# One core, threshold attention and a GELU MLP: eight sums moved forward, one transpose for two heads, and three small moves

## The chip, the cores and the metric

The kernel runs on one core of a Trainium2 chip. A core has a matrix engine (TensorE, PE in the profile; its weight loads are PEld and overlap the matmuls), VectorE (DVE), ScalarE (ACT), GpSimd (POOL), SyncE (SP, which here only issues transfers), and 16 DMA engines that move data between DRAM and the on-chip memories SBUF and PSUM (TensorE writes only to PSUM). Each engine works through its own queue in order, and semaphores hold an instruction back until what it needs is there. The metric is device time in microseconds, as a median of several executions.

## The reference

Inputs are q, k, v of 8 batches x 8 heads x 576 rows x 64, a scalar tau, and two weight matrices.

```python
scores = scale * np.matmul(q, k.transpose(0, 1, 3, 2))        # scale = 1/8
thresh = np.max(scores, axis=-1, keepdims=True) - tau
scores = np.where(scores >= thresh, scores, -1000000000.0)
attn = np.exp(scores - np.max(scores, axis=-1, keepdims=True))
attn = attn / (np.sum(attn, axis=-1, keepdims=True) + 1e-09)
attn_out = np.matmul(attn, v)
x = attn_out.transpose(0, 2, 1, 3).reshape(4608, 512)         # tokens x (head, channel)
h = x @ w_in                                                  # w_in 512 x 2048
g = 0.5 * h * (1.0 + erf(h / sqrt(2)))
out = g @ w_out                                               # w_out 2048 x 512
```

The two weight matrices arrive as 8-byte floats, and the kernel itself brings them to 4 bytes. All matmuls are in 4-byte floats.

## The kernel before, in words

**Slots.** The attention is cut into 32 pairs of heads (four pairs are a batch), and each pair into five chunks of 128 query rows (the fifth has the last 64 rows of both heads). A (pair, chunk) is a slot; there are 160, numbered n. The first 20 slots are the "early" ones: pairs 0 to 3 with chunks 0 and 1 first (n below 8), then chunks 2 to 4 of the same pairs. After them each pair runs through its five chunks. The engines' queues are written out by hand in this order; no scheduler reorders them.

What a slot does: TensorE makes the scores (L355); VectorE takes each row's maximum (L367, reading PSUM); GpSimd forms the threshold (L368); ScalarE the exponential (L370); VectorE compares, multiplies and sums (L386). An early slot then forms reciprocals of the row sums (L389 on GpSimd, L397 on VectorE), puts them on diagonals (L400, ScalarE), and TensorE turns the probabilities by multiplying with these diagonals (L301, one slot later). A later slot turns them on VectorE, in 32 x 32 blocks, with one instruction for each head (L433), into the tiles pd[0] and pd[1], and SyncE's transfers regroup these blocks (L444 for the tail, L448). Divisors are turned by VectorE, sent to DRAM and fetched back, spread over the partitions ("turned", "inv", L408 to L421). TensorE multiplies the turned probabilities with v (L460), one pair later, and VectorE divides while it takes the result out of PSUM (L478).

**The weights' conversion.** There are 32 pieces of 128 x 512. A piece is fetched by GpSimd's queue in two transfers (raw, L154, and the same shifted by three bytes, L156). VectorE takes out the exponent (expo, L176), ScalarE makes a power of two from it (L177), and VectorE does three more steps (mant L183, power L185, and L187, which writes w_in or w_out and behind which the next piece's load is issued). The steps are a generator; VectorE works at one piece's expo ahead of the piece before it. At the end of each slot it goes on until a budget in ns is used up: 3000 in each of the first 8 slots, 3650 up to slot 18, and all that is left in slot 19. Two pieces are loaded before the first slot, two more behind the first chunk of pairs 0 and 1. Odd pieces are fetched into free room of pd[0] and pd[1], even ones into tiles of the pool xg.

**The MLP.** Tokens go in 18 blocks of 256. The first ten are done plainly: h in PSUM (L520), GELU (L500, before which ScalarE loads the GELU table; L507 is a small Exp that brings the Exp table back), the second product (L532), a copy (L535) and a store (L537). Their matmuls fill the slots' gaps on TensorE, by a running goal of blocks done.

**The last eight blocks** are done behind the last slot as four duos, two blocks each, by Strassen's scheme in Winograd's form: 7 products of half-size blocks (L641) instead of 8, with sums and differences of quarters formed by VectorE. The weights' sums come in two parts. `weights_in` (L592 to L594) makes twelve sums out of w_in when the last slot is done, into tiles that are free by then. `strassen`, called when the last pair's products with v and all plain blocks are in the queues, begins with four differences that overwrite quarters of w_in (L612), and then with the four sums of the first duo's tokens (`x_sums`, L653 to L656). Those overwrite the quarter b12 of the second block, and write three new tiles (x_ext). Then, for each of eight chunks of the hidden dimension, TensorE makes the products of the w_in side and VectorE and ScalarE take them out. w_out's quarter sums (L661 to L664) are made inside the first duo. The second products follow, and their results are stored 128 rows x 512 columns at a time (L744, L749) by SyncE. Results are put together in lo (tiles of tag o_sb, n1's rows) and hi (o_ext, n2's rows); each holds two column halves, finished at different times.

**The front.** The program's last part begins with the transfers of pairs 0 and 1: `load_early` puts q's on SyncE's queue and k's, for these two pairs, on ScalarE's, which then turns to L278 and L280, where it copies the turned q and k out of PSUM. The first Exp table is loaded by ScalarE in front of L278.

Of the kernel before, what the change touches and what calls it, by code (L numbers as in the profile page):

```python
# [18 lines left out]
def kernel(  # L19
# [69 lines left out]

    ident = const.tile([P, P], FP32, name="ident")  # L90
# [5 lines left out]
    pd = [const.tile([P, 4 * KR, P], FP32, name=f"pd{e}") for e in range(2)]  # L96
# [326 lines left out]
    def turn_p(p, i):  # L423

        s = st[p]
        w = s.pop(("p", i))
        n = 1 if i == NC else 2  # L430
        for e in reversed(range(n)):
            to = pd_tail[p % 2] if i == NC else pd[e][:, :, i * Q:(i + 1) * Q]
            nc.vector.transpose(to[:, 0:NB, :], w[:, e * S:(e + 1) * S].rearrange("p (b i) -> p b i", i=Q))  # L433
# [58 lines left out]
    warm = const.tile([P, 2], FP32, name="warm")  # L492
    nc.vector.memset(warm, 0.0)

# [15 lines left out]
    def block_steps(n):  # L510

        g = {}
        for j in range(N_DF):
# [11 lines left out]
        for m in range(TOK // P):  # L525
            for j in range(N_DF):
                yield NS_OUT, len(pieces) - N_DF + j + 1
                if j not in g:
                    gelus(0)
                if j == 0:  # L530
                    o = ps.tile([P, 512], FP32, tag="mm", name="o_ps")
                nc.tensor.matmul(o[:, 0:d_model], lhsT=g[j][:, m * P:(m + 1) * P], rhs=w_out_sb[j],  # L532
                                 start=(j == 0), stop=(j == N_DF - 1))
# [5 lines left out]
    mlp = {"n": 0, "steps": None, "next": None, "debt": 0.0}  # L539
# [41 lines left out]
    def weights_in():  # L581
# [3 lines left out]
        rest = [units(v_sb[i % 4])[0] for i in range(NP - 4, NP - 1)]  # L585
# [9 lines left out]
        return (s1, s2, s4), room + rest  # L595
# [11 lines left out]
    def strassen(ext, room):  # L607
        s1, s2, s4 = ext
        for h in range(HF // U):
            for c in range(NK):  # L610
                a = w_in_sb[c][:, HF + h * U:HF + (h + 1) * U]
                vec.tensor_tensor(a, w_in_sb[c][:, h * U:(h + 1) * U], a, op=ALU.subtract)  # L612
        room = room + units(v_sb[(NP - 1) % 4]) + [u for t in pd_tail for u in units(t)]
        room += [x for _ in range(2) for x in unit(xg, "x", 2)]
        x_ext = [room.pop().rearrange("p (c t) -> p c t", c=NK) for _ in range(3)]
# [33 lines left out]
        def x_sums(n1, n2):  # L649
            t1, t2, t4 = x_ext  # L650
            a, b = x_blk[n1], x_blk[n2]
            b11, b21, b12, b22 = a[:, 0:NK, :], a[:, NK:2 * NK, :], b[:, 0:NK, :], b[:, NK:2 * NK, :]
            vec.tensor_tensor(t1, b12, b11, op=ALU.subtract)  # L653
            vec.tensor_tensor(t2, b22, t1, op=ALU.subtract)
            vec.tensor_tensor(b12, b22, b12, op=ALU.subtract)  # L655
            vec.tensor_tensor(t4, b21, t2, op=ALU.subtract)  # L656

# [7 lines left out]

        def finish_chunk(j, x, p3):
# [6 lines left out]
        x_sums(*DUOS[0])  # L673
        for sb, (n1, n2) in enumerate(DUOS):
# [45 lines left out]
            for m in ms:  # L720
# [3 lines left out]
                vec.tensor_tensor(lo[m][:, 0:HD], lo[m][:, 0:HD], vs[m], op=ALU.add)  # L724
            for n in DUOS[sb + 1] if sb + 1 < len(DUOS) else ():
                if n in away:
                    bring(n)
            if sb + 1 < len(DUOS):
                x_sums(*DUOS[sb + 1])
# [7 lines left out]
            for m in ms:  # L737
                product(ys[m], rows(g22, m, wt4))
                vec.tensor_tensor(hi[m][:, 0:HD], hi[m][:, 0:HD], ys[m], op=ALU.add)
            for m in ms:  # L740
                product(xs[m], rows(gs1, m, wt1))
                vec.tensor_tensor(hi[m][:, HD:2 * HD], hi[m][:, HD:2 * HD], xs[m], op=ALU.add)
                row = n2 * TOK + m * P
                nc.sync.dma_start(out[row:row + P, :], hi[m])  # L744
            for m in ms:
                product(xs[m], rows(g12, m, w_out_part(1, 1)))
                nc.scalar.copy(lo[m][:, HD:2 * HD], xs[m])
                row = n1 * TOK + m * P
                nc.sync.dma_start(out[row:row + P, :], lo[m])  # L749

    load_early(0)
    load_early(1)
# [32 lines left out]
    for n in range(len(slots) + WEIGH + 1):  # L785
# [60 lines left out]
        convert(3000 if n < 2 * HP else 3650 if n < BATCH - 1 else 1e9)  # L846
# [54 lines left out]
```

## Time and profile before

| | |
|---|---|
| median of 7 executions | 1430.25 us (1425.93 to 1433.08) |
| the profiled execution | 1426.63 us, of which 1424.5 is its span |
| mean granted clock of TensorE in it | 0.993 |
| TensorE busy | 1379.0 us, 97% of the span |
| VectorE busy | 899.3 us, 63% |
| ScalarE busy | 639.8 us, 45% |
| GpSimd busy | 387.1 us, 27% |
| chain that ended last | TensorE 84%, VectorE 7%, ScalarE 5%, DMA 2% |
| VectorE's transposes, L433 | 224 of 128 x 576, mean 756 ns, 160.7 us |
| VectorE's maxima, L367 | 288, mean 748 ns |
| ScalarE's table loads | 1283 ns each |

How to read it: times are of one execution, in microseconds from the start of the span unless marked ns. In a row, `out<-in` are the program's tile names, then come partitions x elements and the type; `x2` counts merged instructions of one form, which may overlap in time. A bracket such as `[3.24 <-DVE x L655]` is the time that the engine stood idle in front of the row, and what ended it. "Waits" are idle times summed by what ended them. The slices are fortieths of the span, 35.6 us each, and their digits are tenths. A share is a mean over stages with different limits, so what an edit is worth has to be read at its own place.

### The profile page before, as it was taken

Reading aid. Unit: us, or ns where it says so; the run is one execution under the profiler, and the core shown is the slowest. Engines: PE = TensorE matmul, PEld = TensorE weight load, DVE = VectorE, ACT = ScalarE, POOL = GpSimd, SP = SyncE. Lnnn points to the kernel's source line nnn. Section 1 sums busy time; section 2 is a strip of 40 time slices with the busy share of each in tenths; the row PEclk is TensorE's granted clock in tenths of the full one; section 3 lists DMA queues with packets and bytes.
Section 4 is the critical chain, followed back from the end, with each engine's and each line's share of the span. In section 5 each row is a group of like instructions: output and inputs, shape, how many; then the busy total and the mean of one; then the engine's idle time right before and its main releaser. Section 6 shows DMA issues by size and latency. Waiting matters only on the chain.

```text
span 1424.5 us, 19776 instructions
## 1 busy us (share of the span) xinstructions
PE 1379.0 (97%) x6544; PEld 956.9 (67%) x6544; DVE 899.3 (63%) x1908; ACT 639.8 (45%) x1039; POOL 387.1 (27%) x810
## 2 busy tenths in 40 slices
PE   5898899999999999999999999999999999999999
PEld 4676557466475564655746657466488888888887
DVE  5987687777767777777777777777664142241330
ACT  5768535446255373562735627457141141230320
POOL 4443244343334434334334344330000000000000
PEclk8999999999999999999999999999999999999999
DMA  9978267776667776677767777765500100100000
GB/s 267 294 264 241 55 142 150 154 144 126 136 142 143 155 139 140 141 142 162 155 136 144 161 157 149 142 134 101 107 0 1 45 1 0 60 1 8 23 1 30
DMA packets 449492, 167.06 MB, mean 117 GB/s; under 512 B 413040, under 2 KB 432048, under 8 KB 449392
## 3 DMA queue, kind: packets, MB, share of 16 engines
q1 hardware_dynamic: 423184, 108.65, 39.0%
q0 software_dynamic: 23808, 56.57, 13.2%
q8 instruction: 53, 0.87, 0.3%
q10 hardware_dynamic: 2400, 0.59, 0.2%
q14 instruction: 47, 0.39, 0.1%
HBM read 71.68 MB, written 11.47 MB: 58 GB/s over the span
## 4 chain that ended last, share of the span: by engine, by line
PE 84%; DVE 7%; ACT 5%; DMA 2%; issue 1%; SPq 0%; POOL 0%; DVEq 0%; ACTq 0%; POOLq 0%
PE bank L641 27%; PE hT L520 18%; PE o_ps L532 18%; PE sc L355 12%; PE xT L460 9%; DVE p L386 2%; ACT p L370 2%; DVE nmx L367 1%; DVE power L185 1%; ACT L500 1%; DVE w_in L187 1%; ACT diag L400 1%; DVE expo L176 1%; DVE mant L183 0%; PE tr L301 0%
## 5 line engine op out<-in xcount | busy, mean ns | idle before, releaser
L370 ACT ACTIVATE p<-sc,nmx 128x576 f32<-128x576 f32 x288 | 202.3, 738 | 384.2 <-DVE nmx L367 384.1
L367 DVE TENSOR_REDUCE nmx<-sc 128x1 f32<-128x576 f32 x288 | 204.8, 748 | 146.6 <-PE sc L355 146.6
L520 PE MATMUL hT<-x,w_in 128*128 128x256 f32 x1280 | 296.2, 384 | 0.0
L532 PE MATMUL o_ps<-w_out,g 128*128 128x512 f32 x640 | 294.2, 602 | 0.0
L520 PEld LDWEIGHTS hT<-x,w_in 128*128 128x128 f32 x1280 | 238.4, 190 | 56.9 <-issue 25.2
L386 DVE SCALAR_TENSOR_TENSOR p<-sc,thr,p 128x576 f32<-128x576 f32 x288 | 225.2, 815 | 65.4 <-ACT p L370 64.3
L368 POOL TENSOR_SCALAR thr<-nmx,tau_eff 128x1 f32<-128x1 f32 x288 | 84.1, 292 | 545.2 <-DVE nmx L367 542.6
L532 PEld LDWEIGHTS o_ps<-w_out,g 128*128 128x128 f32 x640 | 116.6, 190 | 140.3 <-issue 138.6
L355 PE MATMUL sc<-kT,qT 64*128 64x288 f32 x960 | 164.9, 432 | 2.6 <-DVE p L386 2.3
L460 PE MATMUL xT<-pT,v 128*64 128x288 f32 (+2 forms) x1280 | 164.0, 409 | 3.2 <-ACT g L500 3.2
L433 DVE STREAM_TRANSPOSE pd<-p 128x576 f32<-128x576 f32 x224 | 160.7, 756 | 3.0
L355 PEld LDWEIGHTS sc<-kT,qT 64*128 64x128 f32 x960 | 93.1, 187 | 84.3 <-issue 71.8
L460 PEld LDWEIGHTS xT<-pT,v 128*64 128x64 f32 x1280 | 89.9, 137 | 73.2 <-issue 13.1
L232 POOL DMA_DIRECT2D v<-in_v_dram x208 | 110.5, 534 | 10.5 <-issue 9.5
L641 PE MATMUL bank<-x,w_in 128*128 128x256 f32 x384 | 94.5, 382 | 3.2 <-DVE x L655 3.2
L500 ACT ACT_TABLE_LOAD x71 | 91.1, 1283 | 1.2
L507 ACT ACT_TABLE_LOAD x71 | 91.1, 1283 | 1.2
L641 PE MATMUL bank<-unit 128*128 128x256 f32 x352 | 88.4, 381 | 0.0
L641 PEld LDWEIGHTS bank<-x,w_in 128*128 128x128 f32 x384 | 73.4, 191 | 14.0 <-issue 4.1
L223 POOL DMA_DIRECT2D q<-in_q_dram x104 | 70.6, 684 | 15.7 <-issue 14.8
L641 PEld LDWEIGHTS bank<-unit 128*128 128x128 f32 x352 | 67.4, 192 | 9.4
L641 PE MATMUL bank<-w_out,unit 128*128 128x256 f32 x320 | 72.3, 379 | 0.0
(143 smaller groups left out, 1316.9 us busy)
## 6 DMA issues: line engine op xcount, KB each, us to landing
pT<-pd SPq DMA_DIRECT2D x448, 160.0 KB, 3.9
pT<-pd_tail SPq DMA_DIRECT2D x112, 80.0 KB, 2.8
q<-in_q_dram POOLq DMA_DIRECT2D x104, 72.0 KB, 4.0
k<-in_k_dram POOLq DMA_DIRECT2D x104, 72.0 KB, 2.6
out_dram<-o_sb SPq DMA_DIRECT2D x28, 256.0 KB, 3.9
inv<-turned SPq DMA_DIRECT2D x56, 128.0 KB, 4.1
v<-in_v_dram POOLq DMA_DIRECT2D x156, 40.0 KB, 3.1
raw<-in_moe_w_in_dram POOLq DMA_DIRECT2D x8, 512.0 KB, 6.4
```

Of the source, the lines that this page charges most:

```text
L232: eng.dma_start(t[r:P:4, e, 0:n, :], rows[:, r * KR:r * KR + n, :])
L355: nc.tensor.matmul(sc[e][:, h, 0:HALF], lhsT=lhsT, rhs=s["kT"][rows, at:at + HALF], start=True, stop=True)
L367: nc.vector.tensor_reduce(nmx[:, e:e + 1], sc, axis=AXIS.XY, op=ALU.max, negate=True)
L370: nc.scalar.activation(w[:, e * S:(e + 1) * S].rearrange("p (h s) -> p h s", h=2), sc, AF.Exp, bias=nmx[:, e:e + 1], scale=1.0)
L386: nc.vector.scalar_tensor_tensor(row, sc[e][:, :, 0:HALF], thr[:, e:e + 1], row, op0=ALU.is_ge, op1=ALU.mult, accum_out=den[e])
L433: nc.vector.transpose(to[:, 0:NB, :], w[:, e * S:(e + 1) * S].rearrange("p (b i) -> p b i", i=Q))
L460: nc.tensor.matmul(xT[f, 0:hi - lo], lhsT=s["v"][:, e, c, :], rhs=pT[:, c, lo:hi], start=(c == 0), stop=(c == KR - 1))
L500: nc.scalar.activation(t, hT, AF.Gelu)
L507: nc.scalar.activation(warm[:, 1:2], warm[:, 0:1], AF.Exp)
L520: nc.tensor.matmul(hT[:, j % 2, :], lhsT=w_in_sb[c][:, j * P:(j + 1) * P], rhs=x_blk[n][:, c, :], start=(c == 0), stop=(c == N_DM - 1))
L532: nc.tensor.matmul(o[:, 0:d_model], lhsT=g[j][:, m * P:(m + 1) * P], rhs=w_out_sb[j], start=(j == 0), stop=(j == N_DF - 1))
L641: nc.tensor.matmul(to, lhsT=l, rhs=r, start=start and k == 0, stop=k == len(pairs) - 1, skip_group_check=not start)
```

## The change

Five edits:

1. `pd[0]` and `pd[1]` become two views of one tile, `turned_p`, and `turn_p` turns both heads by one VectorE instruction over 128 x 1152 instead of two over 128 x 576 (the fifth chunk, with one, stays).
2. The four differences that overwrite quarters of w_in and the first duo's four token sums move from the beginning of `strassen` into `weights_in`, directly behind its twelve sums. The tiles x_ext are taken from v's tiles of three of the last four pairs instead of from the end of the list of free room. An assertion says that the last plain block is by then in its second product, so that nothing still reads w_in. `x_sums` becomes a function of its own.
3. A small Exp, with which its table is loaded, is put on ScalarE's queue between the transfers of pair 0 and those of pair 1; the tile that it uses is set to zero at the very beginning.
4. The conversion's budget is 0 in slot 0 and 3400 in slots 1 to 7 (before: 3000 in slots 0 to 7).
5. In `strassen` each result is stored in two halves of 256 columns, each as soon as it is complete, instead of one row block of 512 columns.

```diff
+    warm = const.tile([P, 2], FP32, name="warm")
+    nc.vector.memset(warm, 0.0)
...
-    pd = [const.tile([P, 4 * KR, P], FP32, name=f"pd{e}") for e in range(2)]
+    turned_p = const.tile([P, 2, 4 * KR, P], FP32, name="turned_p")
+    pd = [turned_p[:, e, :, :] for e in range(2)]
...
-        n = 1 if i == NC else 2
-        for e in reversed(range(n)):
-            to = pd_tail[p % 2] if i == NC else pd[e][:, :, i * Q:(i + 1) * Q]
-            nc.vector.transpose(to[:, 0:NB, :], w[:, e * S:(e + 1) * S].rearrange("p (b i) -> p b i", i=Q))
+        if i == NC:
+            nc.vector.transpose(pd_tail[p % 2][:, 0:NB, :], w[:, 0:S].rearrange("p (b i) -> p b i", i=Q))
+            return
+        nc.vector.transpose(
+            turned_p[:, :, 0:NB, i * Q:(i + 1) * Q], w.rearrange("p (e b i) -> p e b i", e=2, i=Q))
...
     def weights_in():
...
-        rest = [units(v_sb[i % 4])[0] for i in range(NP - 4, NP - 1)]
+        x_ext = [units(v_sb[i % 4])[0].rearrange("p (c t) -> p c t", c=NK) for i in range(NP - 4, NP - 1)]
...
-        return (s1, s2, s4), room + rest
...
-    def strassen(ext, room):
-        s1, s2, s4 = ext
+        assert mlp["n"] == PLAIN and mlp["layer"] == 2
         for h in range(HF // U):
             for c in range(NK):
                 a = w_in_sb[c][:, HF + h * U:HF + (h + 1) * U]
                 vec.tensor_tensor(a, w_in_sb[c][:, h * U:(h + 1) * U], a, op=ALU.subtract)
+        x_sums(x_ext, *DUOS[0])
+        return (s1, s2, s4), x_ext, room
...
+    def strassen(ext, x_ext, room):
+        s1, s2, s4 = ext
...
-        x_ext = [room.pop().rearrange("p (c t) -> p c t", c=NK) for _ in range(3)]
...
+        def store(n, m, t, at):
+            row = n * TOK + m * P
+            nc.sync.dma_start(out[row:row + P, at:at + HD], t[:, at:at + HD])
...
-        x_sums(*DUOS[0])
...
                 vec.tensor_tensor(lo[m][:, 0:HD], lo[m][:, 0:HD], vs[m], op=ALU.add)
+                store(n1, m, lo[m], 0)
...
                 vec.tensor_tensor(hi[m][:, 0:HD], hi[m][:, 0:HD], ys[m], op=ALU.add)
+                store(n2, m, hi[m], 0)
...
                 vec.tensor_tensor(hi[m][:, HD:2 * HD], hi[m][:, HD:2 * HD], xs[m], op=ALU.add)
-                row = n2 * TOK + m * P
-                nc.sync.dma_start(out[row:row + P, :], hi[m])
+                store(n2, m, hi[m], HD)
...
                 nc.scalar.copy(lo[m][:, HD:2 * HD], xs[m])
-                row = n1 * TOK + m * P
-                nc.sync.dma_start(out[row:row + P, :], lo[m])
+                store(n1, m, lo[m], HD)
 
     load_early(0)
+    nc.scalar.activation(warm[:, 1:2], warm[:, 0:1], AF.Exp)
     load_early(1)
...
-        convert(3000 if n < 2 * HP else 3650 if n < BATCH - 1 else 1e9)
+        convert(0 if n == 0 else 3400 if n < 2 * HP else 3650 if n < BATCH - 1 else 1e9)
```

## The prediction

> **What bounds the kernel now.** I read the page's forty slices first, then the waits of TensorE, then the order of time around the two places where TensorE stands. All durations are of the profiled execution, 1426.63 us with a span of 1424.5; it lies 3.6 us under the median of the seven runs (1430.25). The sum is made on 1426.63 and the 3.6 is added back at the end. A change of less than 0.2%, 2.9 us, is about what a measurement of this kernel cannot tell from none.
>
> The slices of the page, tenths of busy time and of the granted clock:
>
> ```profile
> PE   5898899999999999999999999999999999999999
> DVE  5987687777767777777777777777664142241330
> PEclk8999999999999999999999999999999999999999
> ```
>
> TensorE is full from slice 6 on; VectorE is at 9 only in the first slices. The table of 25 us windows says the same: VectorE 23.36 us of 25 in 50 to 75 us, some 19 from 200 to 1000. So what saves VectorE time after 200 us saves nothing, unless TensorE is seen waiting. The waits of TensorE from 200 us to the end:
>
> ```profile
> PE bank L641 <- DVE x L655: 3.2, 1, 3.2
> PE xT L460 <- ACT g L500: 3.2, 2, 1.6
> PE bank L641 <- DVE pd L697: 2.1, 4, 0.5
> PE sc L355 <- DVE p L386: 1.4, 6, 0.2
> ```
>
> Of 9.9 us, only the first line is touched by the change.
>
> **The quarter sums.** The timeline where the last pair ends:
>
> ```profile
> 1019.19 0.69 DVE L594 TENSOR_TENSOR unit<-w_in,unit 128x512 f32<-128x512 f32 x1
> ...
> 1024.82 0.95 DVE L478 TENSOR_TENSOR x<-xT,inv 128x64 f32<-128x64 f32 x4 [4.93 <-DMA inv<-turned]
> ...
> 1025.68 2.48 DVE L612 TENSOR_TENSOR w_in<-w_in 128x512 f32<-128x512 f32 x4
> ...
> 1029.42 0.69 DVE L655 TENSOR_TENSOR x<-x 128x512 f32<-128x512 f32 x1
> ...
> 1030.25 2.04 PE L641 MATMUL bank<-x,w_in 128*128 128x256 f32 x4 [3.24 <-DVE x L655]
> ...
> 1032.09 1.71 PE L641 MATMUL bank<-unit 128*128 128x256 f32 x4
> ...
> 1034.50 1.03 PE L641 MATMUL bank<-x,w_in 128*128 128x256 f32 x4
> ```
>
> VectorE ends the weight sums at 1019.9, stands 4.93 us for the divisors' transfer, divides, and only then makes the four differences of w_in (L612, 2.48 us) and the four token sums (L653 to L656, from 1028.09 to 1030.7, 2.6 us). TensorE's second product waits for L655. The change puts these eight operations behind L594: 1019.9 + 2.5 + 2.6 = 1025.0. The one TensorE needs is over at 1024.3, and TensorE asks for it at 1026.9, so 2.6 us are to spare. They lie in the 4.93 us that VectorE stood still; the four divisions behind them start at 1025.0 instead of 1024.8, and the PSUM banks that they free are asked for again only in the second chunk, after 1031. TensorE loses no 3.24 us. It also loses no slow stretch: after the gap four matmuls took 2.04, then 1.71 us, against 1.03 later. By starts, 1030.25 to 1033.64 holds eight matmuls, 3.39 us, where eight of the steady rate take 1.72 (0.86 from start to start of four): 1.67 more. Term: 3.2 + 1.7 = **-4.9 us**, between -3.2 (the slow stretch comes anyway) and -5.2. What is late next is the steady loop, in which each of the rows above is under 0.5 us.
>
> The Trainium skill, "TensorE: Matmul & The Clock Gate", section "What's actually happening", gives half clock after at least one idle window of about 3.4 us. The gap here is 3.24 us and the rows behind it run at half rate; read strictly the rule would leave the clock alone and the whole sum would be 1.7 us smaller. The row decides.
>
> **No conversion in slot 0.** The timeline of the front:
>
> ```profile
> 16.94 0.69 DVE L185 SCALAR_TENSOR_TENSOR power<-raw,power 128x512 uint32<-128x512 uint32 x1 [1.48 <-ACT power L177]
> ...
> 20.17 0.43 DVE L176 TENSOR_SCALAR expo<-raw 128x512 uint32<-128x512 uint32 x1 [1.81 <-DMA raw<-in_moe_w_in_dram]
> ...
> 20.93 1.40 DVE L367 TENSOR_REDUCE nmx<-sc 128x1 f32<-128x576 f32 x2
> ...
> 25.14 0.61 POOL L154 DMA_DIRECT2D raw<-in_moe_w_in_dram  x1
> ...
> 30.81 0.44 DVE L176 TENSOR_SCALAR expo<-raw 128x512 uint32<-128x512 uint32 x1
> ```
>
> VectorE waits 1.48 and 1.81 us inside slot 0's conversions, and slot 1's scores, ready at about 15.9 (L355, 14.89 + 1.31), are first read at 20.93. Without the conversions L367 of slot 1 starts at 15.9, five us earlier. Slot 1's softmax takes 20.93 to 24.38, 3.45 us: 19.35. Then the 3400 of slot 1 are eight steps: expo, expo, mant, power, w_in, expo, mant, power. Starts lie 0.34, 0.34, 0.34, 0.61, 0.69, 0.34, 0.34, 0.61 apart, 3.6 us, and some 0.3 of waiting for ScalarE: slot 2's L367 at 23.3, against 27.71. That is 4.4 us early, but five steps (w_in, expo, mant, power, w_in: 2.7 us) are still owed that were done before: 1.7 ahead.
>
> Now the loads. Piece 4 was issued inside slot 1 (25.14, landed 4.6 us later, a number of the DMA view for that issue) and used at 30.81, unwaited. In the changed program three loads stand together behind slot 2's L389 on GpSimd, piece 4 first, and VectorE wants piece 4 at the end of the same slot. Slot 2's softmax ends at 23.3 + 3.1 = 26.4 (27.71 to 30.81 before), L389 takes 0.6, issue at 27.1, landing at 31.7. VectorE arrives after w_in, expo, mant, power, w_in at 29.1 and stands **2.6 us**; queued behind it are slot 2's reciprocal and slot 3's maximum, and ScalarE's diagonal and TensorE's transposes wait for these. Slot 3's L367 starts at 32.3 against 33.60: 1.3 early, with expo, mant, power and w_in (2.0 us) owed. These are paid in slots 3 to 7, where VectorE has no room (23.36 of 25 us). Term: **+0.7 us**. Bounds: without the stand, -1.9; with the slowest landing of such a load in the front (8.9 us, issue at 46.22), +5.0. I take 4.6 because the loads with 7 to 9 us stood in line behind another piece, which piece 4 would not.
>
> **Table at the front.** One load and its small Exp move ahead of pair 1's three k loads on ScalarE's queue.
>
> ```profile
> 6.21 1.28 ACT L278 ACT_TABLE_LOAD   x1 [6.21 <-DMA k<-in_k_dram]
> ...
> 7.51 0.69 ACT L278 ACTIVATE qT<-tr,q_scale 128x512 f32<-128x512 f32 x1
> 8.28 0.58 ACT L280 COPY kT<-tr 128x512 f32<-128x512 f32 x1
> ```
>
> L278 may start at 7.39 instead of 7.51, but L280 waits for TensorE's transposes until 8.26 either way: 0. Pair 1's k goes out 1.5 us later (4.0 instead of 2.5); its last part, behind q's loads as before, lands near 14.5, when the scores' banks come free (14.45). 0, between -0.1 and +1.
>
> **One transpose for two.** 112 pairs of 1.44 us (mean 756 ns, overlapping) become 112 of 1.2 to 1.5; a 512-wide one takes 678 ns, so the price goes with the elements. On VectorE after 160 us this is covered by TensorE. SyncE's first regroup load of a group now waits for both halves, 0.7 us. In a steady pair sixteen loads run without a gap (207.9 to 224.2), the last tail load is out at 227.4, landed at about 230, and TensorE's second half of L460 starts at 234.7: covered by over 4 us. Only in the last pair (sixteen from 997.6 to 1013.6, tail out at 1017.9, second half at about 1019.9) nothing is to spare: +0.3, between 0 and +0.7.
>
> **Stores by halves.** Sixteen more issues on an idle SyncE. Only the last counts: 128 KB instead of 256 KB.
>
> ```profile
> out_dram<-o_sb SPq DMA_DIRECT2D x2, 256.0 KB, 2.0
> turned<-turned SPq DMA_DIRECT2D x28, 16.0 KB, 2.0
> ```
>
> By these rows size does not matter and the gain is 0; the bytes of the last store fill two slices of 0.525 us in the DMA view, so half of at most 1.05 is the other end. I take -0.3. "DMA: Bandwidth & Descriptors" of the skill ("Measured") asks for batches of 1 MiB and more, which speaks against halves; the sum is the same by it, since no other store is on the path.
>
> **Sum:** -4.9 + 0.7 + 0 + 0.3 - 0.3 = -4.2: 1422.4 on the profiled execution, 1426.0 in the median's frame.
>
> **The rivals.** *A, the front pays too.* Piece 4 lands before VectorE asks for it, because the piece ahead left the queue free. For it: 1.48 + 1.81 us of idle time are really gone. Against: 27.1 + 4.6 is after 29.1. Then -1.9 instead of +0.7: 1423.4. *B, the front is starved.* The DMA engines are at 1.04 and 0.94 of their time from 25 to 75 us, and loads that start later land later (7.1 and 8.9 us are in the rows). Then +3 to +5 instead of +0.7, and 1428.3 to 1430.3: no change to tell. *C, slower: the wide transpose.* If one pattern over both heads costs more per element, VectorE, which has 6 of 25 us free, some 1.5 us a slot, fills up. It decides from 1.44 + 1.5 = 2.9 us; at 3.2 each of 112 slots adds 0.3 and TensorE waits in L355: +34 - 4, about 1460. For it: no row shows this shape; against: the rate of the rows goes with the elements. *D, the sums do not help,* because the compiler's waits hold L655 back to the divisions: 1426.0 + 4.9 = 1430.9; against: nothing they read is written by the divisions.
>
> **How the numbers follow.** My case 0.46, A 0.18, B 0.22, C 0.08, D 0.06. The likeliest case alone reaches from 1424 to 1428. The range 1421.0 to 1431.0 takes in A less 2.4 us of scatter, and B and D whole; C and the tails, some 0.15, are left out. Faster by over 0.2% (under 1427.4): 0.85 of mine (0.39), A, a little of B (0.03): 0.60. Within: the rest of mine (0.07), most of B (0.14), D (0.06): 0.27. Slower (over 1433.1): C, and 0.05 of B, should several loads land late: 0.13.
>
> **What would show it.** Right: no wait for the token sums at the first block products and no matmuls at half rate there (PE at 1.03 us per four at once); slot 1's maximum at about 16 us; a wait of 2 to 3 us for raw at about 29 to 32; slot 3's maximum at 32 to 33. Wrong: slot 8's maximum (65.42 before) more than 2 us away from that; a transpose row over 1.6 us; TensorE waiting between 200 and 1000 us for anything longer than before.

## The result and the profile after

The changed kernel takes 1435.2 us (median of 16 executions, 1432.67 to 1442.02) where the kernel before takes 1429.46 (40 executions): a ratio of 1.0046, 95% interval [1.0037, 1.0055], which is 6.6 us slower (the two medians lie 5.7 us apart). The prediction was 1426.0, at least 1421 and at most 1431: faster than before.

The profiled execution took 1433.68 us, its span 1431.9. It lies 1.5 us under its kernel's median, the profile of before (1426.63) 2.8 us under 1429.46, so what is read between the two profiles is 1.3 us larger than between the medians. The slices of the page after, for the three engines' rows that the prediction showed:

```profile
PE   6898899999999999999999999999999999999999
DVE  4887777777777777777777767777754132241330
PEclk9899999999999999999999999999999999999999
```

Nothing is seen at this grain but a VectorE that is less full at the front. The waits of TensorE from 200 us to the end say more:

```profile
PE sc L358 <- DVE p L389: 4.6, 8, 1.8
PE xT L464 <- ACT g L501: 3.2, 2, 1.6
PE bank L655 <- DVE turned_p L705: 2.1, 4, 0.5
PE xT L464 <- DMA pT<-pd_tail: 0.9, 1, 0.9
PE xT L464 <- issue: 0.6, 1, 0.6
```

The wait for the token sums (3.2 us) is gone, as forecast. New are 3.2 us more of waiting for scores' banks, and 1.5 us for the last pair's tail. Where the time went is best read from when each slot's first maximum starts (L367 before, L370 after), after less before:

| slot (pair, chunk) | us |
|---|---|
| 1 (0, 1) | -2.2 |
| 3 (1, 1) | +2.2 |
| 8 (0, 2) | +6.6 |
| 107 (21, 2) | +6.4 |
| 110 (22, 0) | +8.1 |
| 125 (25, 0) | +8.4 |
| 130 (26, 0) | +11.0 |
| 159, the last | +10.7 |
| end of the span | +7.4 |

So the end gained 3.3 us, and 10.7 were lost before it: 6.6 in the first eight slots, and the rest, in two jumps, in pairs 21 and 25. Of the 6.6 a part is scatter: three kernels below with the front of the kernel before untouched (sums_only, turn_only, halves_only) start slot 8 at 66.9 to 67.3 us, where the profile of before has 65.42.

The timeline of the front, after:

```profile
16.26 0.36 PE L286 MATMUL tr<-ident,k 64*128 64x64 f32 x1 [1.41 <-DMA k<-in_k_dram]
...
18.69 1.42 DVE L370 TENSOR_REDUCE nmx<-sc 128x1 f32<-128x576 f32 x2 [3.80 <-PE sc L358]
...
25.86 1.40 DVE L370 TENSOR_REDUCE nmx<-sc 128x1 f32<-128x576 f32 x2
...
35.38 0.43 DVE L179 TENSOR_SCALAR expo<-raw 128x512 uint32<-128x512 uint32 x1 [3.72 <-DMA raw<-in_moe_w_in_dram]
...
35.80 1.40 DVE L370 TENSOR_REDUCE nmx<-sc 128x1 f32<-128x576 f32 x2
```

TensorE's queue waits for pair 1's k before it comes to slot 1's scores; VectorE, with no conversions to do, stands 3.80 us. It stands again, 3.72 us, for the piece whose load was forecast to be late.

The jump in pair 21, on SyncE and VectorE, before and then after:

```profile
685.11 0.59 SPq L413 DMA_DIRECT2D turned<-turned  x1
687.05 0.60 SPq L419 DMA_DIRECT2D inv<-turned  x1
...
693.27 0.52 DVE L478 TENSOR_TENSOR x<-xT,inv 128x192 f32<-128x192 f32 x2 [0.87 <-DMA inv<-turned]
```

```profile
693.30 0.58 SPq L416 DMA_DIRECT2D turned<-turned  x1
697.35 0.59 SPq L422 DMA_DIRECT2D inv<-turned  x1
...
703.62 0.52 DVE L482 TENSOR_TENSOR x<-xT,inv 128x192 f32<-128x192 f32 x2 [4.78 <-DMA inv<-turned]
...
707.51 1.42 DVE L370 TENSOR_REDUCE nmx<-sc 128x1 f32<-128x576 f32 x2
```

Taken from the pair's slot, the store of pair 20's divisors is issued 1.8 us later than before (693.30 less 685.11 and less the 6.4 of the front), their fetch 3.9 us later. VectorE's division waits 4.78 us, and behind it on its queue stand the transpose and the next slot's maximum, for which TensorE waits. The table of 200 to 1000 us (busy us of the engines, then granted clock, the 16 DMA engines' busy share, GB/s) has the same bytes moved in both, but not in the same time; before and then after:

```profile
200.00:1000.00 800.00, 795.38 (x3713) 487.77 (x3712) 604.19 (x1240) 407.31 (x540) 308.31 (x637) 1.00 0.71 143
```

```profile
200.00:1000.00 800.00, 792.09 (x3674) 485.18 (x3673) 594.06 (x1128) 403.85 (x538) 308.50 (x637) 1.00 0.77 144
```

The share went from 0.71 to 0.77: the transfers themselves became slower. No step of the prediction has a place for that.

### The profile page after: what moved, and what is told of

It is laid out like the page before. It is cut to its first block, busy times and chain, and to the rows that moved or that the text cites. A ratio compares the mean times of both kernels' runs of the same rounds, so it can differ in the third digit from the quotient of the medians.

```text
span 1431.9 us, 19665 instructions
## 1 busy us (share of the span) xinstructions
PE 1384.7 (97%) x6544; PEld 959.3 (67%) x6544; DVE 892.2 (62%) x1796; ACT 639.9 (45%) x1040; POOL 386.8 (27%) x810
## 4 chain that ended last, share of the span: by engine, by line
PE 83%; DVE 7%; ACT 5%; DMA 3%; issue 1%; SPq 1%; POOL 0%; DVEq 0%; ACTq 0%; POOLq 0%
PE bank L655 27%; PE hT L522 17%; PE o_ps L535 17%; PE sc L358 12%; PE xT L464 9%; ACT p L373 2%; DVE p L389 2%; PE tr L304 1%; DVE nmx L370 1%; DVE power L188 1%; ACT L501 1%; DMA k<-in_k_dram 1%; DVE w_in L190 1%; ACT diag L403 1%; DMA turned<-turned 1%
## 5 line engine op out<-in xcount | busy, mean ns | idle before, releaser
L370 DVE TENSOR_REDUCE nmx<-sc 128x1 f32<-128x576 f32 x288 | 204.8, 748 | 136.8 <-PE sc L358 136.6
L436 DVE STREAM_TRANSPOSE turned_p<-p 128x1152 f32<-128x1152 f32 x112 | 154.1, 1376 | 3.2 <-DVE x L482 0.2
L235 POOL DMA_DIRECT2D v<-in_v_dram x208 | 110.6, 534 | 10.7 <-issue 10.0
L655 PE MATMUL bank<-x,w_in 128*128 128x256 f32 x384 | 93.3, 379 | 0.0
L655 PE MATMUL bank<-w_out,unit 128*128 128x256 f32 x416 | 92.4, 379 | 0.0
L655 PEld LDWEIGHTS bank<-w_out,unit 128*128 128x128 f32 x416 | 79.0, 190 | 10.7
L655 PEld LDWEIGHTS bank<-x,w_in 128*128 128x128 f32 x384 | 73.0, 190 | 10.3 <-issue 0.5
L304 PE MATMUL tr<-diag,p 128*128 128x128 f32 (+1 forms) x360 | 50.5, 306 | 22.9 <-ACT diag L403 13.9
```

The lines of the kernel that those rows point to most:

```text
L235: eng.dma_start(t[r:P:4, e, 0:n, :], rows[:, r * KR:r * KR + n, :])
L370: nc.vector.tensor_reduce(nmx[:, e:e + 1], sc, axis=AXIS.XY, op=ALU.max, negate=True)
L436: nc.vector.transpose(turned_p[:, :, 0:NB, i * Q:(i + 1) * Q], w.rearrange("p (e b i) -> p e b i", e=2, i=Q))
L655: nc.tensor.matmul(to, lhsT=l, rhs=r, start=start and k == 0, stop=k == len(pairs) - 1, skip_group_check=not start)
```

## The experiments

All ratios are to the kernel before, timed in the same session, with 95% intervals; differences in us are worked out from the ratio. "Share" is the busy share of the 16 DMA engines from 200 to 1000 us.

### Each part alone

**sums_only**: the eight sums moved, nothing else.

```diff
-        return (s1, s2, s4), room + rest
+        for h in range(HF // U):
+            ...  (the four differences of w_in, from strassen)
+        x_sums(x_ext, *DUOS[0])
+        return (s1, s2, s4), x_ext, room
```

> The kernel before, with the four differences and the first duo's token sums moved behind the twelve weight sums, and nothing else. Theory (the parts' effects are separate, and the changed kernel's loss lies elsewhere): no wait for the token sums in front of the first block products and no matmuls at half rate there, -4 to -5 us, ratio 0.9965 to 0.9972; the distance from the last pair's first maximum to the end of the span shrinks by as much. Rival (the eight sums crowd out something of the last pair, whose tail is seen 1.5 us later in the changed kernel): -3.4 us or less, and TensorE waits for the regrouped tail there, as in the changed kernel (0.9 us for pd_tail).

0.9972 [0.9959, 0.9985], -4.0 us. The wait for L655 is gone, the first eight products run at full rate (1.89 us for eight), and from the last slot's maximum to the end of the span there are 411.6 us instead of 416.6: -5.0. The rival's crowding is not there: the last 40 products with v run in one row.

**slot0_only**: no conversion in slot 0.

```diff
-        convert(3000 if n < 2 * HP else 3650 if n < BATCH - 1 else 1e9)
+        convert(0 if n == 0 else 3400 if n < 2 * HP else 3650 if n < BATCH - 1 else 1e9)
```

> The kernel before, with no conversion in slot 0 and 3400 in slots 1 to 7. Theory (two causes in the front: the fifth piece's load is issued too late, and the table's place makes pair 1's k late): the k part is missing here, so slot 1's maximum starts at 16 to 17 us and not at 18.7; VectorE still stands 3 to 4 us for the fifth piece in slot 2; slot 8's maximum 3.5 to 4.5 us later than before, the time +3.5 to +4.5 us, ratio 1.0025 to 1.0031. Rival (all of the front's loss is the missing conversion, the table costs nothing): slot 8 6 us later, ratio 1.004 or more.

1.0031 [1.0016, 1.0046], +4.4 us. Slot 1's maximum starts at 16.23, slot 8's at 71.22, 5.8 us behind the profile of before and 4.0 to 4.3 us behind the three unchanged fronts. VectorE's waits from 11.2 us to there (the 6.9 us are for the very first scores; before has 6.84):

```profile
DVE nmx L367 <- PE sc L355: 10.2, 4, 6.9
DVE p L386 <- ACT p L370: 4.3, 8, 1.8
DVE expo L176 <- DMA raw<-in_moe_w_in_dram: 3.3, 1, 3.3
```

**turn_only**: one transpose for both heads, in one tile (the two hunks on `turned_p` and `turn_p`).

```diff
-        for e in reversed(range(n)):
-            ...
+        nc.vector.transpose(
+            turned_p[:, :, 0:NB, i * Q:(i + 1) * Q], w.rearrange("p (e b i) -> p e b i", e=2, i=Q))
```

> The kernel before, with both heads turned by one instruction and nothing else. Theory (the one tile or the one instruction makes the regrouping transfers slower, the divisors of pairs 20 and 24 come too late): the regrouping loads of a pair take 1 to 2 us longer than before, the mean busy share of the DMA engines between 200 and 1000 us is 0.75 or more (0.71 before), TensorE loses 2 to 4 us there, ratio 1.0015 to 1.003. Rival (the transfers are slower because the front's loss has shifted the slots against the loads of q, k and v, or it is that run's own): share 0.71 to 0.72, no loss between 200 and 1000 us, ratio 0.9995 to 1.0005.

1.0005 [0.9996, 1.0014]; the share is 0.71, nothing is lost between 200 and 1000 us. My theory fell: the merged transpose does not slow the transfers. The instruction takes 1376 ns (154.1 us for 112).

**table_only**: the small Exp between the two `load_early`, with its tile set to zero first.

```diff
+    warm = const.tile([P, 2], FP32, name="warm")
+    nc.vector.memset(warm, 0.0)
     ident = const.tile([P, P], FP32, name="ident")
...
-    warm = const.tile([P, 2], FP32, name="warm")
-    nc.vector.memset(warm, 0.0)
...
     load_early(0)
+    nc.scalar.activation(warm[:, 1:2], warm[:, 0:1], AF.Exp)
     load_early(1)
```

> The kernel before, with the small Exp and its table load put between pair 0's and pair 1's transfers on ScalarE's queue, and nothing else. Theory: pair 1's k tail lands at about 16.2 us as in the changed kernel, but the conversions of slot 0 cover it up to 20.9 us, so slot 1's maximum stays at 20.9 to 21 us; ratio 0.9995 to 1.0005. Rival (the late k also holds up pair 2's loads and what is behind): slot 8's maximum over 1 us later, ratio 1.001 or more.

1.0050 [1.0033, 1.0067], +7.1 us, from the part that was costed at nothing; the rival had the direction, but neither the size nor the place. Slot 8's maximum at 67.87 us is only 0.6 to 1.0 us behind the unchanged fronts, but the share is 0.76, and pairs 21 and 25 lose 2.3 and 3.9 us. A table load at 2.5 us is no likely cause of slower transfers at 700. But the diff does something else: it takes the tile `warm` out of the end of the const tiles and puts it first. In the built program it takes 32 bytes a partition, and all const tiles behind it move up by 32: pd, from which SyncE regroups, starts 128 bytes past a multiple of 256 before, 160 past one after.

### Is it the address?

**table_warm_last** and **warm_first** take the two halves of that part apart; **after_warm_last** is the changed kernel with `warm` allocated behind `w_out_sb`, as **table_warm_last** has it.

```diff
(table_warm_last, after_warm_last; table_warm_last has the Exp of table_only too)
     w_out_sb = [const.tile([P, d_model], FP32, name=f"w_out{j}") for j in range(N_DF)]
+    warm = const.tile([P, 2], FP32, name="warm")
+    nc.vector.memset(warm, 0.0)
(warm_first)
+    warm = const.tile([P, 2], FP32, name="warm")
+    nc.vector.memset(warm, 0.0)
     ident = const.tile([P, P], FP32, name="ident")
...  (in all three the two lines go from their old place)
```

> The kernel before with the table load at the front, as in table_only, but the 32 bytes a partition of the tile warm stand behind all other const tiles again, where they were. Theory (the slow transfers come from the addresses: with warm first, pd, pd_tail and v start 32 bytes further on): the DMA engines' busy share between 200 and 1000 us is 0.71 to 0.73, the pT loads take 3.9 us and not 4.1, no loss in pairs 21 and 25, ratio 0.999 to 1.001 where table_only had 1.005. Rival (the table's place in ScalarE's queue does it, by the order in which the first transfers go out): share 0.76, ratio 1.004 or more.

1.0017 [1.0006, 1.0028], above the theory's range; share 0.72, nothing lost in pair 21, 2.0 us in pair 25; the pT loads take 3.9 us.

> The kernel before with the tile warm and its memset moved to the front of the const tiles, so that those behind it start 32 bytes further on, and nothing else: no table at the front. Theory (addresses): share 0.75 to 0.77, the divisors' loads of pairs 20 and 24 go out 31 us or more behind the pair's third maximum (27.9 and 28.9 before), TensorE loses 2 to 6 us in pairs 21 and 25, ratio 1.003 to 1.006. Rival (the table's place): share 0.72, ratio 0.9995 to 1.0005.

1.0024 [1.0014, 1.0034], less than the theory's 1.003 to 1.006; share 0.76, pairs 21 and 25 lose 1.9 and 2.7 us, pair 23 another 1.3. The pT loads take 4.1 us. No table is moved here, and the slow transfers are back:

```profile
200.00:1000.00 800.00, 791.87 (x3670) 484.78 (x3670) 600.29 (x1230) 406.52 (x539) 308.51 (x637) 1.00 0.76 143
```

> The changed kernel with one edit: the tile warm stands behind all other const tiles, as before the change. Theory (addresses): share between 200 and 1000 us 0.71 to 0.73 (0.76 to 0.77 in the changed kernel), no loss in pairs 21 and 25, ratio to the kernel before 1.000 to 1.002: sums -4, slot 0 +4.4, turn +0.7. Rival (the loss of the changed kernel is the table's or the slots' phase): ratio 1.004 or more.

1.0011 [1.0000, 1.0022] where the changed kernel has 1.0046; share 0.72, nothing lost in pairs 21 and 25:

```profile
200.00:1000.00 800.00, 794.79 (x3686) 487.33 (x3687) 599.85 (x1138) 406.61 (x539) 311.72 (x642) 1.00 0.72 144
```

The three runs say the same: the share follows the tile's place, not the table's. For the time, the shift is worth 0.0024 by itself and 0.0035 in the changed kernel.

The single packets in the traces say which tile it is. From 200 to 1000 us the packets of 256 bytes on SyncE's queue, 10240 a pair, are the pieces that the regrouping reads from pd. They take 21.7 ns on average before and in table_warm_last, 21.9 in after_warm_last, but 23.5 in warm_first, 23.4 in table_only and 23.6 in the changed kernel; that is about three quarters of the rise of the share. The pieces of 128 bytes from pd_tail took longer too (12.6 ns before, 14.3 in warm_first).

Pair 21 costs 1.7 to 2.3 us in the three kernels with the shift, 0.6 in slot0_loads, and nothing in the others. Pair 25 is less clean: it costs 2.6 to 3.9 us with the shift, but also 1.0 to 2.1 in seven of the eleven other kernels with pd where it was before (halves_only and slot0_only among them), and nothing in the five with pd at a multiple of 256 (next). So its margin is thin before the change too; the profile of before is an execution in which it held.

**pd_aligned** and **both_aligned** go the other way.

```diff
(pd_aligned)
+    const.tile([P, 32], FP32, name="pad")
     pd = [const.tile([P, 4 * KR, P], FP32, name=f"pd{e}") for e in range(2)]
(both_aligned, besides)
     w_out_sb = [const.tile([P, d_model], FP32, name=f"w_out{j}") for j in range(N_DF)]
+    const.tile([P, 8], FP32, name="pad2")
```

> The kernel before with an unused tile of 128 bytes a partition ahead of pd, so that pd0 and pd1, from which 256-byte pieces are read for the regrouping, start at a multiple of 256 (before at 128 past one, in the changed kernel at 160 past one); pT, to which they are written, goes from 96 to 224 past one. Theory (a transfer reads whole 256-byte lines, and pieces that straddle two cost more): the DMA engines' share between 200 and 1000 us falls clearly, to 0.50 to 0.65 from 0.72, SyncE issues a pair's divisors 3 us or more earlier, the time falls by 0 to 2 us, since TensorE waits for these transfers hardly anywhere, ratio 0.998 to 1.0005. Rival (only a start off a multiple of 64 costs, or the write side counts as much): share 0.70 to 0.74, no gain.

0.9979 [0.9968, 0.9989], -3.0 us where -2 was the most expected. Share 0.65, divisors fetched 1.7 us earlier on average (3 were expected), no loss in pairs 21 and 25. The 256-byte packets take 18.1 ns. Part of the gain stands at the end: TensorE waits 1.7 us for the token sums, not 3.2, since the divisors come earlier.

> pd_aligned, with 32 unused bytes more behind the weights, so that pT, q and k start at multiples of 256 too. Theory (it is the read side): as pd_aligned, share within 0.02 of it. Rival (the write side counts too): share another 0.03 or more lower than pd_aligned. Time in both cases within 0.1% of pd_aligned.

0.9963 [0.9949, 0.9976], 0.0016 under pd_aligned where 0.001 was expected, with intervals that overlap. From 200 to 1000 us only the transfers differ much from the row of before; the wait for the token sums is 1.3 us:

```profile
200.00:1000.00 800.00, 795.38 (x3713) 488.22 (x3712) 606.12 (x1242) 408.70 (x542) 309.10 (x639) 1.00 0.61 143
```

The share is 0.61, so the rival holds: where the written tiles start counts too (the 256-byte packets, for which only pT has moved, go from 18.1 to 17.4 ns). That the read side counts held as well, but in size 0.65 is the upper end of what was expected of it. An unused tile of 128 bytes and one of 32 are worth as much as the eight sums.

**halves_only**: the stores by halves.

```diff
-                nc.sync.dma_start(out[row:row + P, :], lo[m])
+                store(n1, m, lo[m], HD)
```

> The kernel before with the last blocks' results stored by halves as soon as each is complete, and nothing else. Theory: only the last store's size counts, -0.5 to 0 us, the last store lands about 0.3 us sooner behind the last copy. Rival (smaller rows of 1 KB make the last stores slower, or the sixteen more issues hold up a transfer that a duo waits for): +0.5 us or more.

0.9996 [0.9983, 1.0008]: not to be told from nothing by the time. By the profile, the span ends 2.7 us behind the last copy's end instead of 3.0.

### The front

**slot0_piece4** and **slot0_loads** ask whether the late load explains slot 0's loss.

```diff
(slot0_piece4, on slot0_only)
             if p < 2:
                 load_piece()
+            if p == 1:
+                load_piece()
...
-                load_piece()
+                if converted[0]:
+                    load_piece()
(slot0_loads, on slot0_only)
-            if p < 2:
+            if p == 0:
+                load_piece()
                 load_piece()
```

> slot0_only, with the fifth piece's load issued behind the first chunk of pair 1 together with the fourth's, instead of behind the first piece's conversion (every piece's conversion but the first then loads the next). Theory (what the missing conversion of slot 0 costs is the wait for the fifth piece): no wait for raw over 1 us in slots 1 to 4, slot 3's maximum at 31 to 33 us, slot 8's maximum 0 to 2 us before that of the kernel before, ratio 0.9985 to 1.0000 where slot0_only had 1.0031. Rival (the DMA engines are full up to 75 us, so the wait only moves to the sixth piece or to q, k and v): a wait of 2 us or more in slots 2 to 6, slot 8 still 3 us or more late, ratio 1.002 or more.

1.0040 [1.0026, 1.0054], which says nothing about the fifth piece: the edit made the fourth piece late instead, and VectorE stood 5.1 us for it and 2.1 for the fifth. It shows only that these waits follow the issue.

> slot0_only, with the load that stood behind the first chunk of pair 1 (slot 2) moved to slot 0, so that slot 0 issues the third and the fourth piece and each conversion from the first on loads the next: the fifth piece goes out at about 20 us, not at 28.7. (slot0_piece4 did not do this: there the fourth piece, left out at the first conversion, waited until slot 2 and went out at 26.4 instead of 20.2.) Theory (the missing conversion costs what its late loads cost): the wait of 3.3 us for the fifth piece in slot 2 goes, none over 1.5 us takes its place, slot 8's maximum is 2 to 4 us earlier than in slot0_only, ratio 0.999 to 1.001. Rival (the DMA engines are full up to 75 us and a load issued earlier lands no sooner, or it takes the time from q, k and v of pairs 1 to 3): waits of 2 us or more for raw, pd, or for scores in slots 1 to 6, ratio 1.002 or more.

1.0018 [1.0007, 1.0030], between the two ranges. The wait for the piece is gone, VectorE has none of 2 us or more in its place, and slot 3's maximum starts at 29.79, 3.8 us before the profile of before. But at slot 8 it is 2.6 us behind it, 0.8 to 1.1 us behind the other unchanged fronts. In between, on TensorE and VectorE:

```profile
38.23 0.16 DVE L397 RECIPROCAL den<-den 128x2 f32<-128x2 f32 x1
...
39.28 4.41 PE L301 MATMUL tr<-diag,p 128*128 128x128 f32 x20 [3.35 <-ACT diag L400]
```

The reciprocal stands behind the conversion steps; TensorE waits 3.35 us for the diagonals and then takes 4.41 us for twenty transposes that take 2.42 in a slot of the changed kernel without such a wait (at 52.45 us). The granted clock from 25 to 75 us is 0.84 (0.95 before, 0.93 to 0.97 in the unchanged fronts). The length of such a wait alone does not decide: in slot0_only twenty transposes take 2.42 us behind waits of 3.22 and 2.94 us, and 4.41 behind one of 2.60.

**slot0_loads_3000** (budget 0 in slot 0, 3000 in slots 1 to 7) and **budget_3400** (3000 in slot 0, 3400 in slots 1 to 7) separate the budget from the missing slot.

```diff
(slot0_loads_3000, with slot0_loads' loads)
+        convert(0 if n == 0 else 3000 if n < 2 * HP else 3650 if n < BATCH - 1 else 1e9)
(budget_3400)
+        convert(3000 if n == 0 else 3400 if n < 2 * HP else 3650 if n < BATCH - 1 else 1e9)
```

> slot0_loads with the budget of slots 1 to 7 at 3000 instead of 3400, so that the conversions left out in slot 0 are made after slot 7. Theory (the larger budget puts one more step ahead of the reciprocal in some slots, TensorE waits over 3 us for the diagonals there and goes on at half rate): TensorE's longest wait for a diagonal between 25 and 75 us is under 2.6 us (3.3 in slot0_loads), the granted clock there 0.92 or more (0.84), slot 8's maximum at 61 to 64 us, ratio 0.998 to 1.0003. Rival (the missing conversion itself, whatever the budget): longest wait 3 us or more, clock under 0.88, slot 8 at 65 us or later, ratio 1.001 or more.

1.0012 [1.0001, 1.0023]. The longest wait for a diagonal is 1.9 us, the clock 0.91, slot 8 at 63.44 us: by these the theory holds, the clock just short of its 0.92. By the time it does not, and this is why: slot 19, where all that is left is converted, now has three pieces instead of two and takes 13 us instead of 5. TensorE's waits from 150 to 200 us:

```profile
PE tr L301 <- ACT diag L400: 7.1, 1, 7.1
```

> The kernel before with 3400 instead of 3000 in slots 1 to 7 only; slot 0 converts as before. Theory (the larger budget): longest wait for a diagonal between 25 and 75 us 3 us or more (2.4 before), clock 0.90 or less, slot 8's maximum at 69 us or later (65.4 to 67.3 in the kernels with the old front; 2.8 us more of conversions are made by then), ratio 1.000 to 1.002. Rival: longest wait under 2.6 us, clock 0.93 or more, slot 8 at 68 to 70 us by the added steps alone, ratio 0.9985 to 1.000, since those steps are missing later.

1.0000 [0.9987, 1.0013]. Longest wait 3.1 us, clock 0.87, slot 8 at 69.72 as in the theory; then the steps made early are missing later, and by slot 25 the 2.5 us lost to sums_only's front are 0.2. So the larger budget does starve TensorE, but alone it costs nothing in the end; the conversion left out in slot 0 costs, wherever its steps are paid.

### What the parts come to

**after_two_undone**: the changed kernel with `warm` last and the budget of before.

```diff
-        convert(0 if n == 0 else 3400 if n < 2 * HP else 3650 if n < BATCH - 1 else 1e9)
+        convert(3000 if n < 2 * HP else 3650 if n < BATCH - 1 else 1e9)
(and warm behind w_out_sb)
```

> The changed kernel with two edits undone: the tile warm stands behind the other const tiles, and the conversion's budget is 3000 in slots 0 to 7. The eight sums, the merged transpose, the table at the front and the stores by halves stay. Theory (the two account for the loss, the parts add): sums -4.2, turn +0.7, table without the shift +2.4, halves -0.6: -1.7 us, ratio 0.9980 to 0.9995, faster than the kernel before. Rival (something else in the changed kernel costs too, or the table's 1.0017 was front noise): ratio over 1.000, or under 0.9975.

0.9974 [0.9963, 0.9985], 1425.91 us: faster than before, and within 0.1 us of what was predicted for the whole change, which is luck: that sum had +0.7 for slot 0, which is undone here. It lies just in the rival's range: the table, the merged transpose and the halves cost nothing here that can be seen beside the sums' 0.9972. The three ratios in a row, 0.9974, 1.0011 (after_warm_last, slot 0 changed) and 1.0046 (the shift too), put the loss half on the one and half on the other.

**after_aligned**: after_warm_last with the unused tiles of both_aligned.

> The changed kernel with the tile warm behind the other const tiles and with the unused tiles of both_aligned, so that pd (both heads) and pT start at multiples of 256; slot 0 still converts nothing. Theory (the front's loss lies in slots 0 to 7, where the regrouping doesn't run yet, so alignment does not mend it; pairs 21 and 25 lose nothing): slot 8's maximum 70 to 73 us, ratio 0.9985 to 1.0000. Rival (both losses are late transfers in general): slot 8's maximum under 69 us and ratio under 0.997.

0.9989 [0.9976, 1.0002]. Slot 8's maximum at 72.88 us: alignment does not mend the front. Share 0.62, nothing lost in pairs 21 and 25.

**sums_aligned** and **sums_halves_all_aligned** look for the best version. The second has the 128 bytes ahead of ident and 128 more ahead of the pool xg.

```diff
(both_aligned with sums_only's edit; then, for the second, halves_only's too and)
+    const.tile([P, 32], FP32, name="pad")
     ident = const.tile([P, P], FP32, name="ident")
...
+    small.tile([P, 32], FP32, tag="pad", name="pad3", bufs=1)
```

> both_aligned with the eight sums moved behind the twelve weight sums. Theory: both_aligned (0.9963) still waited 1.3 us for the token sums where the kernel before waited 3.2, so the sums bring less here: -2 to -3 us more, ratio 0.9938 to 0.9950. Rival (the gains are separate and add): 0.9935 or less.

0.9954 [0.9939, 0.9969], 1423.17 us: another 0.0009 on both_aligned's 0.9963, less than the theory's 0.0013 to 0.0025, with intervals too wide to tell.

> sums_aligned with the stores by halves, and with the unused 128 bytes ahead of ident instead of ahead of pd and 128 more ahead of the pool xg, so that v, the tokens' blocks, raw and o_sb start at multiples of 256 as well. Theory: these transfers are few beside the regrouping, -1 to 0 us against sums_aligned. Rival (the raw pieces' landing sets the front): the conversions' waits for raw and pd in slots 0 to 3 shrink by 2 us or more, and the time falls by 1 to 3 us.

0.9950 [0.9934, 0.9965], 1422.62 us, the fastest kernel of this study: 6.9 us under the kernel before in the same runs (1429.53), 12.6 under the changed one. Between 200 us and the end, TensorE waits in it only for the GELU (two waits, 3.2 us), in the steady loop (2.1) and 1.4 us in all for scores, the same as in sums_only's profile.

## Why the prediction was wrong, step by step

- **Quarter sums (-4.9).** Right: -5.0 from last slot to end in sums_only's profile, -4.0 by its time. The half-rate stretch went with the gap (eight matmuls in 1.89 us). From 1020 to 1050 us the granted clock is 1.00 there and was 0.94 before. The prediction had set its row, half rate behind a gap of 3.24 us, against the idle window of about 3.4 us that the Trainium skill, "TensorE: Matmul & The Clock Gate", section "What's actually happening", gives; the row was right. In the changed kernel the same end gained only 3.3, for the tail of the last pair came late; the timeline after:

```profile
1031.41 0.67 PE L464 MATMUL xT<-pT,v 128*64 128x288 f32 x2 [0.90 <-DMA pT<-pd_tail]
...
1034.80 0.68 DVE L624 TENSOR_TENSOR v<-x,v 128x512 f32<-128x512 f32 x1
1037.63 0.95 DVE L482 TENSOR_TENSOR x<-xT,inv 128x64 f32<-128x64 f32 x4 [2.15 <-DMA inv<-turned]
1038.73 1.89 PE L655 MATMUL bank<-x,w_in 128*128 128x256 f32 x8
```

  The sums end at 1035.5, TensorE starts the blocks at 1038.73 without a wait for them. It waits 0.9 us for the tail instead, and 0.6 us for nothing that the profile shows. Most of this loss goes with the shift: with the tile `warm` last again, from the last slot to the end takes 412.0 us (after_warm_last), against 413.4 in the changed kernel and 411.6 in sums_only, and no wait for the tail is left.

- **Table at the front ("0, between -0.1 and +1").** This is the step that failed by mechanism: a term put at nothing. It costed the instructions and their places in the queues, and not what the same lines do to the allocation: a tile made first moves every const tile behind it. warm_first, with the allocation alone, is 1.0024; table_only with both is 1.0050. Of the forecast's own mechanism, pair 1's late k, the step said "lands near 14.5": it landed at 16.2, 1.7 us later, and is hidden only while slot 0 converts (in table_only slot 1's maximum stays at 20.81 us, in the changed kernel VectorE stands 3.80 us for it).

- **No conversion in slot 0 (+0.7, between -1.9 and +5.0).** Right mechanism, mis-sized term: +4.4. The stand for the fifth piece was 3.3 us (2.6 forecast; 3.7 in the changed kernel, where k was late too); its load went out at 28.71 instead of 27.1 and took 4.8 us. Slot 3's maximum came at 33.99 instead of the 32.3 worked out. (Slot 1's scores, "ready at about 15.9", are at 16.2 by the two numbers beside it, and slot 1's maximum came at 16.23.) What the step had far too small was the debt: "2.0 us" owed at slot 3, charged once. From slot 3's maximum to slot 8's are 37.2 us in slot0_only and 31.3 to 33.1 before and in the unchanged fronts, so 4.2 to 6.0 more. Slots 3 to 7 do not simply take VectorE's steps end to end: the reciprocal, diagonals and transposes stand behind them, TensorE waits 13.6 us for diagonals from 25 to 75 us (7.6 before) and goes on at a lower clock (0.86, 0.95 before). How much of the loss is the waits and how much the clock was not separated. Rival A (the load in time) was built in slot0_loads, and it did not gain: 1.0018.

- **One transpose for two (0, +0.3 in the last pair).** Right within what can be measured: 1.0005; 1376 ns lie in the forecast's 1.2 to 1.5 us. Rival C did not happen.

- **Stores by halves (-0.3).** 0.27 us by the profile of halves_only; the time can't show it.

- **The rivals.** B, the starved front, had the right size for slot 0 for the wrong reason (the late load took 4.8 us, not 7 to 9), and half of the loss was in no rival: each of them moved a wait, none the duration of the regrouping's transfers. The test named in the prediction ("TensorE waiting between 200 and 1000 us for anything longer than before") is the one that caught it: 1.8 us for scores, where 0.2 was the longest.

What stays open: the front's scatter between executions (65.4 to 67.3 us at slot 8 with the same instructions) is as large as the table's own cost, so 1.0017 for table_warm_last is not explained. No run shifts one tile alone; that pd counts most rests on the packets.

## What to carry to other kernels

A line that allocates is part of a change: before costing an edit at nothing, compare the start addresses of all tiles that transfers touch. Where many small transfers run, let their tiles start at multiples of 256 bytes, the best of the starts that were tried here; the busy share of the DMA engines shows it, long before the time does. Work that fills a wait is not free to move: here each conversion step left out of slot 0 came back where its cover was thinner.

## What the runs showed of the hardware

The DMA engines' share from 200 to 1000 us, with the same bytes, by where pd (read, in pieces of 256 bytes) and pT (written) start past a multiple of 256: 0.76 to 0.77 at 160 and 96; 0.71 to 0.72 at 128 and 96; 0.65 at 0 and 224; 0.61 to 0.62 at 0 and 0. TensorE never waits for most of these transfers; it is the thin margins, pairs 21 and 25 and the last pair, that turned this into time.

The Trainium skill, "DMA: Bandwidth & Descriptors", section "How a descriptor splits into AXI transactions", says that a read starts at a 256-byte boundary and that the bytes ahead of the piece cost beats. Worked out from it, an estimate: 8 beats for an aligned piece of 256 bytes, 12 at 128 past, 13 at 160 past. The runs agree in direction. From 128 to 160 (before and warm_first, pT unmoved) the packets took 8% longer, 21.7 to 23.5 ns, as the beats do. From 128 to 0 (pd_aligned) they took 17% less, 18.1 ns, half of the 33% that the beats lose, though pT moved there too. The section speaks of reads alone. Between pd_aligned and both_aligned only the written side of these packets moved, and they took another 4% less (17.4 ns); the tail's pieces of 128 bytes went from 14.3 to 12.6 ns. So the writes count as well, and by what rule is open.
